# Gate and value of a SwiGLU block as 64-row products, one in each half of the PE array, issued in turn

## The chip, the cores and the metric

One Trainium2 chip, one of its cores. The metric is the time that the device takes for one execution of the program, in microseconds (us), the median of several runs.

## What is computed

The reference is an mLSTM cell over 4 batches, 8 heads, 768 tokens and 40 elements a head, and a SwiGLU block over the 3072 tokens of 320 elements that come out of it (8 heads x 40). All is fp32. Cut to what matters:

```python
for t in range(S):                                   # S = 768, in every batch and head
    m_new = np.maximum(f_gate[:, :, t] + m, i_gate[:, :, t])
    f_stab = np.exp(f_gate[:, :, t] + m - m_new)
    i_stab = np.exp(i_gate[:, :, t] - m_new)
    m = m_new
    C = f_stab * C + i_stab * outer(v[t], k[t])
    n = f_stab * n + i_stab * k[t]
    denom = np.maximum(np.abs(n @ q[t]), 1.0)
    y[:, :, t] = sigmoid(o_gate[:, :, t]) * (C @ q[t]) / denom

x = y.transpose(0, 2, 1, 3).reshape(3072, 320)
g = x @ w_gate                                       # 320 x 1536
out = (g * sigmoid(g) * (x @ w_val)) @ w_out         # 1536 x 320
```

The weights of the block come as fp64 and are rounded to fp32 on the chip.

## The kernel before

**The cell.** The 768 tokens of a batch are six chunks of 128. A chunk of a batch is a unit u, so there are 24, and a unit goes through five stages. `turn` (from L242) loads a later unit's k, q, v and o, and transposes k and q on TensorE (tp_kq, eight transposes, two tiles), which ACT copies to SBUF (kT, qT). Two heads lie in the two halves of the partitions, 64 rows each. `scores` (L256) multiplies kT and qT head by head: four matmuls with the lower 64 rows into one tile sp, then four with the upper 64 into another, each tile then weighted by DVE (s_sb). `attend` (L266) makes inter, add and intra and the state C. `rows` (L300) works out the denominators (den) on DVE and x_sb, the 128x320 output of the cell for the chunk: POOL multiplies (L310), DVE divides (L311). `seam` (L313) transposes x_sb on TensorE into tp_x, in three pieces of 128, 128 and 64 columns, and copies it into xT, whose partitions are then the 320 elements in chunks of 128, 128 and 64 (`kch`, L53): the first two pieces on ACT, the third on DVE (L324).

Before the first unit of a batch, `weigh` (L222) makes the weights between tokens: 48 matmuls of 32 rows (nm), DVE, a select on POOL, an exponential on ACT.

**The block.** A step `hidden(b, n, m)` (L334) makes 128 of the 1536 columns for half a batch (384 tokens): gate, three matmuls that add up in one PSUM tile gv_ps (128, 128 and 64 rows of the weights, 384 columns of xT), then value, three more in another gv_ps. ACT takes the sigmoid of the gate (L345), DVE multiplies twice (L346, L347) into h_sb. Twelve such steps make a half batch, then three steps `project` (L349), twelve matmuls each (o_ps), a copy on ACT and a store. So there are 96 hidden steps and 24 projections. A matmul of fp32 is recorded as two weight loads and two matmuls.

**The order.** The first batch's cell runs first, and between its stages the weights of the block come in (L212 to L217): 24 pieces, each a DMA and a chain of five DVE operations, one of ACT and an add on POOL (L209), which turns fp64 into fp32. Then each batch's 30 steps of the block run with the 30 stages of the next batch's cell among them, one after each step (L377 to L389); the last batch's steps run alone. A tile framework builds the program from this: it may move instructions on an engine, and sets the waits between engines.

**PSUM.** Eight banks, two for each of four tags: tr (tp_g, dec, tp_kq, tp_x), att (nm, sp), hp (inter, add, intra) and gen (gv_ps, o_ps).

Of the kernel before, what the change touches and what calls it, by code (L numbers as in the profile page):

```python
# [9 lines left out]
F32 = mybir.dt.float32  # L10
# [6 lines left out]
L = 128  # tokens of a chunk  # L17
# [4 lines left out]
def kernel(  # L22
# [24 lines left out]
    PR = H // 2  # pairs of heads, a head in each half of the partitions  # L47
# [5 lines left out]
    kch = [(d0, min(128, DM - d0)) for d0 in range(0, DM, 128)]  # L53
    NKC = len(kch)
    assert NB * L == S and NFC * 128 == DF and TW % 128 == 0 and TW <= 512 and D <= DP and BH <= 128
# [7 lines left out]
    psum = ctx.enter_context(tc.tile_pool(name="psum", bufs=2, space=PSUM))  # L63
# [47 lines left out]
    # which pair a row of the gates belongs to, and which half  # L111
# [6 lines left out]
    # a pair's state is kept whole; a head's own part of it is its half's columns  # L118
# [27 lines left out]
    # token on the partition: g_T[t, c, bh] and, for the chunks from the second, e_T  # L146
    g_T = const.tile([128, NB, BH], F32)
    e_T = const.tile([128, NB, BH], F32)
    for dst, src, c0 in ((g_T, g_sb, 0), (e_T, e_sb, 1)):
        tp = psum.tile([128, NB, BH], F32, name="tp_g", tag="tr")  # L150
# [4 lines left out]
    # the decay of a whole chunk, spread over the partitions of the state  # L155
# [3 lines left out]
    dec_ps = psum.tile([128, NB - 1, B * PR], F32, name="dec_ps", tag="tr")  # L159
# [8 lines left out]
    conv_scope = ExitStack()  # L168
    conv = conv_scope.enter_context(tc.tile_pool(name="conv", bufs=2))
    PW = 512  # L170
    NPW = max(PW, 2 * DM)

    def weight(dst, src):
        if src.dtype == F32:
            nc.scalar.dma_start(out=dst, in_=src)
            return
# [30 lines left out]
        if len(shape) == 3:  # L207
            sz, tf = (x.rearrange("p (a d) -> p a d", a=shape[1]) for x in (sz, tf))
# [211 lines left out]
```

## Time and profile before

| | us |
|---|---|
| median of 3 runs | 925.11 (924.93 to 929.82) |
| span of the profiled execution | 925.1 |
| PE busy | 875.6 |
| DVE busy | 337.9 |
| ACT busy | 156.1 |
| POOL busy | 120.8 |

The profile is that of one execution. PE is TensorE's matmuls, PEld its weight loads, which can lie under matmuls. A matmul's end is modelled, so that rows of neighbouring matmuls overlap by up to 0.2 us: durations in the timeline are best taken from start to start. The chain is followed back from the last instruction, each time to what released it. In rows of stages (windows) a pair such as 17.35 (x24) is busy time and records of PE, then of PEld where the row is of one source line, and the last three numbers are the granted share of TensorE's clock, the mean busy share of the DMA engines, and GB/s.

### The profile page before, as it was taken

To read this page: it belongs to the slowest core of one execution; us is meant where nothing else is said; L and a number is where in the kernel's file an instruction comes from. 1 tells how busy PE (TensorE), PEld (TensorE's weight loads), DVE (VectorE), ACT (ScalarE), POOL (GpSimd) and SP (SyncE) were. 2 spreads that over 40 slices of the span, in tenths; PEclk is the share of its full clock that TensorE was granted. 3 is DMA by queue.
4 is the path that set the end of the run, shared out by engine and by line. 5 is a ranking of instruction groups with operands and counts; after the bars stand their busy time and mean duration, and the time that the engine had idled before them with its cause. 6 is when DMAs were issued, how large, how long until landed. Compare 5 with 4: busy or idle time off the path is not lost.

```text
span 925.1 us, 8778 instructions
## 1 busy us (share of the span) xinstructions
PE 875.6 (95%) x3477; PEld 553.0 (60%) x3477; DVE 337.9 (37%) x625; ACT 156.1 (17%) x274; POOL 120.8 (13%) x127
## 2 busy tenths in 40 slices
PE   6856769999999999999999999999999999999998
PEld 5755557855665568755665568655755565445445
DVE  5588877433214322334213322234313321210220
ACT  2322122311111112311111112311111101100110
POOL 2344434400000001100000002100000000000000
PEclk9999855599999999799999998799999999999999
DMA  9244454011021111011111110011100000000000
GB/s 139 64 108 112 116 132 114 1 21 30 15 44 21 29 18 33 7 25 27 27 31 22 29 29 22 7 29 22 37 14 1 1 8 14 1 0 22 0 1 21
DMA packets 107273, 32.22 MB, mean 35 GB/s; under 512 B 100640, under 2 KB 103712, under 8 KB 107232
## 3 DMA queue, kind: packets, MB, share of 16 engines
q1 hardware_dynamic: 103392, 19.87, 12.0%
q10 hardware_dynamic: 3840, 11.80, 4.1%
q8 instruction: 27, 0.44, 0.2%
q14 instruction: 14, 0.11, 0.0%
HBM read 27.72 MB, written 3.93 MB: 34 GB/s over the span
## 4 chain that ended last, share of the span: by engine, by line
PE 92%; DVE 3%; issue 1%; DMA 1%; POOL 1%; ACT 0%; ACTq 0%; DVEq 0%; POOLq 0%
PE gv_ps L341 49%; PE o_ps L352 17%; PE nm L230 8%; PE intra L293 5%; PE sp L263 5%; PE inter L273 3%; PE tp_kq L252 3%; PE add L280 2%; PE tp_x L319 1%; DVE top L196 1%; POOL wv_sb L209 0%; DVE size L204 0%; DMA raw<-in_moe_w_gate_dram 0%; DVE top L195 0%; DVE power L203 0%
## 5 line engine op out<-in xcount | busy, mean ns | idle before, releaser
L341 PE MATMUL gv_ps<-xT,wg_sb 128*128 128x384 f32 (+1 forms) x576 | 237.4, 531 | 0.0
L341 PE MATMUL gv_ps<-xT,wv_sb 128*128 128x384 f32 (+1 forms) x576 | 233.5, 526 | 0.0
L341 PEld LDWEIGHTS gv_ps<-xT,wv_sb 128*128 128x128 f32 (+1 forms) x576 | 94.4, 190 | 130.2 <-issue 103.6
L352 PE MATMUL o_ps<-wo_sb,h_sb 128*128 128x320 f32 x576 | 159.3, 435 | 0.0
L341 PEld LDWEIGHTS gv_ps<-xT,wg_sb 128*128 128x128 f32 (+1 forms) x576 | 96.1, 194 | 99.8 <-issue 76.5
L352 PEld LDWEIGHTS o_ps<-wo_sb,h_sb 128*128 128x128 f32 x576 | 108.1, 190 | 44.7 <-issue 1.1
L346 DVE TENSOR_TENSOR sg<-sg,gv_ps 128x384 f32<-128x384 f32 x96 | 53.1, 553 | 221.7 <-ACT sg L345 221.7
L345 ACT ACTIVATE sg<-gv_ps 128x384 f32<-128x384 f32 x96 | 47.1, 490 | 335.7 <-PE gv_ps L341 335.6
L347 DVE TENSOR_TENSOR h_sb<-sg,gv_ps 128x384 f32<-128x384 f32 x96 | 53.2, 554 | 118.8 <-PE gv_ps L341 118.8
L230 PE MATMUL nm<-M_sb,nid 32*128 32x128 f32 x384 | 79.9, 395 | 2.1 <-DVE w_sb L232 1.1
L230 PEld LDWEIGHTS nm<-M_sb,nid 32*128 32x128 f32 x384 | 76.0, 300 | 5.8 <-DVE w_sb L232 3.6
L247 POOL TENSOR_TENSOR v_w<-va,w_sb 128x328 f32<-128x328 f32 x24 | 18.1, 752 | 315.0 <-PE add L280 254.3
L293 PEld LDWEIGHTS intra<-va,s_sb 128*128 128x128 f32 x384 | 54.2, 221 | 3.5 <-issue 0.3
L293 PE MATMUL intra<-va,s_sb 128*128 128x41 f32 x384 | 53.8, 306 | 0.0
L263 PEld LDWEIGHTS sp<-qT,kT 64*128 64x128 f32 x384 | 47.1, 228 | 10.8 <-ACT qT L254 4.8
L263 PE MATMUL sp<-qT,kT 64*128 64x128 f32 x384 | 48.6, 324 | 3.2 <-ACT qT L254 3.2
L232 DVE TENSOR_TENSOR w_sb<-nm,g_T 128x512 f32<-128x512 f32 x48 | 33.2, 691 | 39.6 <-PE nm L230 39.4
L310 POOL TENSOR_TENSOR x_sb<-o_sb,y_sb 128x320 f32<-128x320 f32 x24 | 20.8, 869 | 190.3 <-DVE y_sb L296 187.2
L252 PE MATMUL tp_kq<-ident,kq 128*128 128x128 f32 x192 | 34.1, 323 | 7.3 <-DVE xT L324 5.2
L319 PE MATMUL tp_x<-ident,x_sb 128*128 128x128 f32 (+1 forms) x72 | 14.9, 323 | 25.5 <-DVE x_sb L311 25.5
L252 PEld LDWEIGHTS tp_kq<-ident,kq 128*128 128x128 f32 x192 | 25.5, 164 | 20.6 <-issue 9.9
L234 POOL TENSOR_SCALAR_AFFINE_SELECT w_sb<-w_sb 128x1024 f32<-128x1024 f32 x24 | 26.6, 1108 | 82.5 <-DVE w_sb L232 82.5
(70 smaller groups left out, 494.3 us busy)
## 6 DMA issues: line engine op xcount, KB each, us to landing
kq<-in_k_dram SPq DMA_DIRECT2D x24, 160.0 KB, 3.0
kq<-in_q_dram SPq DMA_DIRECT2D x24, 160.0 KB, 2.8
va<-in_v_dram SPq DMA_DIRECT2D x24, 160.0 KB, 2.6
o_sb<-in_o_gate_dram SPq DMA_DIRECT2D x24, 160.0 KB, 2.6
raw<-in_moe_w_out_dram ACTq DMA_DIRECT2D x6, 640.0 KB, 4.0
out_dram<-z_sb SPq DMA_DIRECT2D x24, 160.0 KB, 1.8
raw<-in_moe_w_gate_dram ACTq DMA_DIRECT2D x6, 512.0 KB, 3.7
raw<-in_moe_w_val_dram ACTq DMA_DIRECT2D x6, 512.0 KB, 3.6
```

The lines of the kernel that those rows point to most:

```text
L230: nc.tensor.matmul(nm[:, j, :], lhsT=nid[:, row:row + 1].to_broadcast([BH, 128]), rhs=M_sb[:, c, :], start=True, stop=True)
L232: nc.vector.tensor_tensor(w[:, two], nm, g2[:, two].unsqueeze(2).to_broadcast([128, PR, L]), op=ALU.add)
L234: nc.gpsimd.affine_select(wf, wf, compare_op=ALU.is_ge, fill=NEG, base=0, pattern=[[0, H], [1, L]], channel_multiplier=-1)
L252: nc.tensor.transpose(tp[:, j, :], un["kq"][:, n, 2 * j:2 * j + 2, :].rearrange("p h d -> p (h d)"), ident)
L263: nc.tensor.matmul(sp[:, j, :], lhsT=un["kT"][r, j, :], rhs=un["qT"][r, j, :], start=True, stop=True)
L273: nc.tensor.matmul(inter[:, 2 * j:2 * j + 2, :].rearrange("p h d -> p (h d)"), lhsT=un["qT"][:, j, :], rhs=state["C"][:, j, :], start=True ...
L293: nc.tensor.matmul(intra[:, h, :], lhsT=un["s"][:, h % 2, h // 2, :], rhs=un["v"][:, h, :], start=True, stop=True)
L341: nc.tensor.matmul(p, lhsT=w_sb[0:dn, kc, ts(m, 128)], rhs=xts[b][0:dn, kc, ts(n, TW)], start=(kc == 0), stop=(kc == NKC - 1))
L345: nc.scalar.activation(sg, ps[0], AF.Sigmoid)
L346: nc.vector.tensor_tensor(sg, sg, ps[0], op=ALU.mult)
L347: nc.vector.tensor_tensor(hs[b, n][:, m, :], sg, ps[1], op=ALU.mult)
L352: nc.tensor.matmul(p, lhsT=hs[b, n][:, m, ts(i, 128)], rhs=wo_sb[:, m, :], start=(m == 0), stop=(m == NFC - 1))
```

## The change

Gate and value are no longer cut in pieces of 128, 128 and 64 rows but in five of 64. The gate's weights lie in partitions 0 to 63 of one tile wgv_sb, the value's in 64 to 127, so that a gate product uses the lower 64 rows of the array and a value product the upper 64. `hidden` takes both PSUM tiles at once and issues the two in turn, five pieces each. For that the tokens must lie in both halves of the partitions: `rows` copies x_sb on POOL into xx_sb, each group of 64 columns twice, and `seam` makes five transposes of 128 columns, in two PSUM tiles of four and one, both copied by ACT. The weights come in 12 pieces for gate and value together (128 partitions x 5 x 128, by two DMAs of 64 partitions each) and six for the third matrix, 18 for 24. PSUM has two tags of four banks: gen as before for gv_ps and o_ps, and cell for all else.

```diff
-    kch = [(d0, min(128, DM - d0)) for d0 in range(0, DM, 128)]
-    NKC = len(kch)
+    HP = 64
+    NKC = DM // HP
...
-    psum = ctx.enter_context(tc.tile_pool(name="psum", bufs=2, space=PSUM))
+    psum = ctx.enter_context(tc.tile_pool(name="psum", bufs=4, space=PSUM))
...
-    wg_sb = wpool.tile([128, NKC, DF], F32)
-    wv_sb = wpool.tile([128, NKC, DF], F32)
+    wgv_sb = wpool.tile([128, NKC, DF], F32)
...
-    PW = 512
-    NPW = max(PW, 2 * DM)
+    PW = 128
+    NPW = max(NKC * PW, 2 * DM)
...
-        for kc, (d0, dn) in enumerate(kch):
-            for sb, dram in ((wg_sb, moe_w_gate), (wv_sb, moe_w_val)):
-                pieces.append((sb[0:dn, kc, f0:f0 + PW], dram[d0:d0 + dn, f0:f0 + PW]))
+        src = [(slice(i * HP, (i + 1) * HP), w[:, f0:f0 + PW].rearrange("(c p) f -> p c f", p=HP))
+               for i, w in enumerate((moe_w_gate, moe_w_val))]
+        pieces.append((wgv_sb[:, :, f0:f0 + PW], src))
...
-            sp = psum.tile([128, PR, L], F32, name="sp", tag="att")
+            sp = psum.tile([128, PR, L], F32, name="sp", tag="cell")
...
+        xx = un["x"] = work.tile([128, NKC, 2, HP], F32, name="xx_sb")
+        nc.gpsimd.tensor_copy(xx, x.rearrange("p (c d) -> p c d", d=HP).unsqueeze(2).to_broadcast([128, NKC, 2, HP]))
...
-        tp = psum.tile([128, NKC, L], F32, name="tp_x", tag="tr")
-        for kc, (d0, dn) in enumerate(kch):
-            nc.tensor.transpose(tp[0:dn, kc, :], units[u]["x"][:, d0:d0 + dn], ident)
-        full = DM // 128
-        nc.scalar.copy(xts[b][:, 0:full, ts(c, L)], tp[:, 0:full, :])
-        if full < NKC:
-            dn = kch[-1][1]
-            nc.vector.tensor_copy(xts[b][0:dn, full, ts(c, L)], tp[0:dn, full, :])
+        for k0, k1 in ((0, 4), (4, NKC)):
+            tp = psum.tile([128, PR, L], F32, name="tp_x", tag="cell")
+            for kc in range(k0, k1):
+                nc.tensor.transpose(tp[:, kc - k0, :], units[u]["x"][:, kc, :, :].rearrange("p a d -> p (a d)"), ident)
+            nc.scalar.copy(xts[b][:, k0:k1, ts(c, L)], tp[:, 0:k1 - k0, :])
...
-        ps = []
-        for w_sb in (wg_sb, wv_sb):
-            p = psum.tile([128, TW], F32, name="gv_ps", tag="gen")
-            for kc, (_, dn) in enumerate(kch):
-                nc.tensor.matmul(p, lhsT=w_sb[0:dn, kc, ts(m, 128)], rhs=xts[b][0:dn, kc, ts(n, TW)],
+        ps = [psum.tile([128, TW], F32, name="gv_ps", tag="gen") for _ in range(2)]
+        for kc in range(NKC):
+            for i in range(2):
+                r = slice(i * HP, (i + 1) * HP)
+                nc.tensor.matmul(ps[i], lhsT=wgv_sb[r, kc, ts(m, 128)], rhs=xts[b][r, kc, ts(n, TW)],
                                  start=(kc == 0), stop=(kc == NKC - 1))
-            ps.append(p)
```

How the built program changes, at three places. First TensorE, from the scores of one unit of the second batch on (x3 means three matmuls; gv_ps is gate and value, of which the first row is the end of the step before). Before:

```order
L341 MATMUL gv_ps<-xT,wv_sb 128x384 x3
L263 MATMUL sp<-qT,kT 128x128 x8
L341 MATMUL gv_ps<-xT,wg_sb 128x384 x3
L341 MATMUL gv_ps<-xT,wv_sb 128x384 x3
L273 MATMUL inter<-C_sb,qT 128x82 x4
L280 MATMUL add<-v_w,kq_84 128x82 x4
L341 MATMUL gv_ps<-xT,wg_sb 128x384
L293 MATMUL intra<-va_87,s_sb 128x41 x8
```

The same stretch and what follows it, up to the next transposes of k and q, after:

```order
L261 MATMUL sp<-qT,kT 128x128 x8
L339 MATMUL gv_ps<-xT,wgv_sb 128x384 x10
L271 MATMUL inter<-C_sb,qT 128x82 x4
L278 MATMUL add<-v_w,kq_84 128x82 x4
L291 MATMUL intra<-va_87,s_sb 128x41 x8
L339 MATMUL gv_ps<-xT,wgv_sb 128x384 x20
L321 MATMUL tp_x<-ident,xx_sb 128x128 x5
L339 MATMUL gv_ps<-xT,wgv_sb 128x384 x10
L250 MATMUL tp_kq<-ident,kq_85 128x128 x8
```

A step is ten matmuls where it was six, no single gate product stands between add and intra any more, and two whole steps lie between intra and the transposes tp_x. With tile numbers, the ten of one step read so (a number is a PSUM tile, so the first is the gate's, the second the value's):

```order
L339 MATMUL gv_ps_1167<-xT_358,wgv_sb_105 128x384
L339 MATMUL gv_ps_1168<-xT_358,wgv_sb_105 128x384
L339 MATMUL gv_ps_1167<-xT_358,wgv_sb_105 128x384
L339 MATMUL gv_ps_1168<-xT_358,wgv_sb_105 128x384
L339 MATMUL gv_ps_1167<-xT_358,wgv_sb_105 128x384
```

Gate and value alternate product by product. In the third step, among the first batch's last stages, the order has five of the gate and then five of the value.

Second TensorE at the start of the program, where the gates are transposed (tp_g) and the first batch is weighed (nm). Before:

```order
L152 MATMUL tp_g<-ident,g_sb 128x32 x6
L230 MATMUL nm<-M_sb,nid 128x128 x11
L152 MATMUL tp_g<-ident,e_sb 128x32 x5
L230 MATMUL nm<-M_sb,nid 128x128
L160 MATMUL dec_ps<-dec_r,halves 128x80
L230 MATMUL nm<-M_sb,nid 128x128 x20
```

After:

```order
L152 MATMUL tp_g<-ident,g_sb 128x32 x6
L152 MATMUL tp_g<-ident,e_sb 128x32 x5
L160 MATMUL dec_ps<-dec_r,halves 128x80
L228 MATMUL nm<-M_sb,nid 128x128 x48
L250 MATMUL tp_kq<-ident,kq_83 128x128 x8
L261 MATMUL sp<-qT,kT 128x128 x8
```

All 48 products of the first weighing now stand behind the transposes of e_sb, and the first transposes of k and q behind all 48; before, they were mixed.

Third POOL, in the first batch's cell, where the adds of the weight pieces (L206, once L209) stand among the cell's operations. Before:

```order
L247 TENSOR_TENSOR v_w<-va_86,w_sb 128x328
L209 TENSOR_TENSOR wg_sb<-top,size 64x512
L288 TENSOR_TENSOR C_old<-C_sb,dec 128x328
L310 TENSOR_TENSOR x_sb<-o_sb,y_sb 128x320
L209 TENSOR_TENSOR wv_sb<-top,size 64x512
```

After:

```order
L245 TENSOR_TENSOR v_w<-va_86,w_sb 128x328
L286 TENSOR_TENSOR C_old<-C_sb,dec 128x328
L308 TENSOR_TENSOR x_sb<-o_sb,y_sb 128x320
L206 TENSOR_TENSOR wgv_sb<-top,size 128x5x128
L311 COPY xx_sb<-x_sb 128x640
```

The copy of x_sb is new, and in this stage an add of a weight piece stands before it on POOL.

More of the change, by code (lines that the diff above doesn't have):

```diff
@@ L249, in turn @@
         for n, name in enumerate(("kT", "qT")):
-            tp = psum.tile([128, PR, L], F32, name="tp_kq", tag="tr")
+            tp = psum.tile([128, PR, L], F32, name="tp_kq", tag="cell")
             for j in range(PR):
@@ L270, in attend @@
         if c > 0:
-            inter = psum.tile([128, H, D1], F32, name="inter", tag="hp")
+            inter = psum.tile([128, H, D1], F32, name="inter", tag="cell")
             for j in range(PR):
@@ L277, in attend @@
         if c + 1 < NB:
-            add = psum.tile([128, PR, 2 * D1], F32, name="add", tag="hp")
+            add = psum.tile([128, PR, 2 * D1], F32, name="add", tag="cell")
             for j in range(PR):
@@ L290, in attend @@
             state["C"] = new
-        intra = psum.tile([128, H, D1], F32, name="intra", tag="hp")
+        intra = psum.tile([128, H, D1], F32, name="intra", tag="cell")
         for h in range(H):
@@ L307, in rows @@
         nc.vector.reciprocal(den, den)
-        x = un["x"] = work.tile([128, DM], F32, name="x_sb")
+        x = work.tile([128, DM], F32, name="x_sb")
         x3 = x.rearrange("p (h d) -> p h d", d=D)
```

26 lines of the change are left out of this document (12 added, 14 removed).

## The prediction

> **What bounds the kernel now.** I read the page first (busy time, the chain that ended last), then the stages in windows, then the timeline of single stages.
>
> ```profile
> span 925.1 us, 8778 instructions
> PE 875.6 (95%) x3477; PEld 553.0 (60%) x3477; DVE 337.9 (37%) x625; ACT 156.1 (17%) x274; POOL 120.8 (13%) x127
> PEclk9999855599999999799999998799999999999999
> PE 92%; DVE 3%; issue 1%; DMA 1%; POOL 1%; ACT 0%; ACTq 0%; DVEq 0%; POOLq 0%
> PE gv_ps L341 49%; PE o_ps L352 17%; PE nm L230 8%; PE intra L293 5%; PE sp L263 5%; PE inter L273 3%; PE tp_kq L252 3%; PE add L280 2%; PE tp_x L319 1%; DVE top L196 1%; POOL wv_sb L209 0%; DVE size L204 0%; DMA raw<-in_moe_w_gate_dram 0%; DVE top L195 0%; DVE power L203 0%
> ```
>
> TensorE is 92% of the chain, and the gate and value products alone (gv_ps) are 49%. The median of the runs is 925.11 us and the profiled span 925.1, so the sum below is made on the span and needs no correction.
>
> The products by stage (PE busy, records, granted clock):
>
> ```profile
> 0.00:186.00 186.00, 17.35 (x24) 6.24 (x24) 0.79 0.44 98
> 771.18:925.10 153.92, 111.61 (x288) 46.62 (x288) 1.00 0.02 8
> ```
>
> A hidden step (one m: gate and value) leaves 12 records, since each fp32 product is recorded as two loads and two matmuls: 2 products x 3 pieces x 2. So 2 of the 96 steps run before 186.00, 24 after 771.18 with no cell among them (288/12), and 70 between, among the cell's stages. Steps between other stages:
>
> ```profile
> 204.06 2.29 PE L341 MATMUL gv_ps<-xT,wg_sb 128*128 128x384 f32 x6
> 208.61 1.10 PE L252 MATMUL tp_kq<-ident,kq 128*128 128x128 f32 x8
> 209.54 2.29 PE L341 MATMUL gv_ps<-xT,wg_sb 128*128 128x384 f32 x6
> 214.00 1.60 PE L263 MATMUL sp<-qT,kT 64*128 64x128 f32 x16
> 215.54 2.40 PE L341 MATMUL gv_ps<-xT,wg_sb 128*128 128x384 f32 x6
> 220.19 1.12 PE L273 MATMUL inter<-C_sb,qT 128*128 128x82 f32 x8
> 771.18 2.29 PE L341 MATMUL gv_ps<-xT,wg_sb 128*128 128x384 f32 x6
> 826.91 19.65 PE L352 MATMUL o_ps<-wo_sb,h_sb 128*128 128x320 f32 x72
> ```
>
> From start to start a step takes 4.55, 4.46 or 4.65 us (204.06 to 208.61, 209.54 to 214.00, 215.54 to 220.19), and the twelve from 771.18 to 826.91 take 55.73, 4.64 each. I use 4.60 for the 70.
>
> **What a record costs.** Two neighbouring looks at the timeline without a change of row count, then three groups of weight loads:
>
> ```profile
> 508.25 0.81 PE L341 MATMUL gv_ps<-xT,wg_sb 128*128 128x384 f32 x2
> 508.57 0.81 PE L341 MATMUL gv_ps<-xT,wg_sb 128*128 128x384 f32 x2
> 240.32 0.29 PEld L341 LDWEIGHTS gv_ps<-xT,wg_sb 64*128 64x128 f32 x2 [0.55 <-issue]
> 241.16 0.94 PEld L341 LDWEIGHTS gv_ps<-xT,wv_sb 128*128 128x128 f32 x4 [0.55 <-issue]
> 242.65 0.29 PEld L341 LDWEIGHTS gv_ps<-xT,wv_sb 64*128 64x128 f32 x2 [0.55 <-issue]
> ```
>
> Undisturbed records start 0.32 us apart; I take 0.322. Where the row count changes, more passes: the two 64-row records take 0.84 (240.32 to 241.16) and the four 128-row records 1.49 (241.16 to 242.65). Together that is 2.33 where six records would be 1.93: a pair of changes, 64 rows in and out, costs 0.40. The idle 0.55 of the weight loader ends at each such change: the load is no longer hidden there. Each step has two such pairs, 0.80 of its 4.64.
>
> **Do two halves run side by side?** The change lives on this. The old trace shows it in the scores, eight matmuls (16 records) of 64 rows, first four in the lower half, then four in the upper. Two short looks:
>
> ```profile
> 512.71 1.60 PE L263 MATMUL sp<-qT,kT 64*128 64x128 f32 x16
> 512.82 0.38 PE L263 MATMUL sp<-qT,kT 64*128 64x128 f32 x2
> 513.37 0.39 PE L263 MATMUL sp<-qT,kT 64*128 64x128 f32 x4
> 514.24 2.40 PE L341 MATMUL gv_ps<-xT,wg_sb 128*128 128x384 f32 x6
> ```
>
> At 513.00 two records are in flight, at 513.55 four, with the same spread of starts (0.38 and 0.39 us with the tail): for a while the halves work at once at full pace, weight loads included. Issued in blocks of eight, they overlap only where the blocks meet; issued in turn, they can overlap all along.
>
> **The change, part by part.**
>
> 1. A step now has 10 products of 64 rows, 20 records, 10 in each half: 10 x 0.322 = 3.22 us if the halves overlap. Row changes are paid only where a run of 64-row work starts and ends. In the new order the 70 steps stand in 47 runs (eight in each twelve steps, one less at the start; scores join the run beside them), the last 24 in 2.
> Among the cells: 70 x 4.60 = 322.0 before; 70 x 3.22 + 47 x 0.40 = 244.2 after: **-77.8**. The last 24: 2 x 55.73 = 111.5 before; 24 x 3.22 + 0.8 = 78.1 after: **-33.4**.
> Bounds: 0.320 to 0.325 a record gives -2 to +3 (96 x 10); a run at 0.20 (only one side is paid) to 0.50 (the second half pays its first load after the first) gives -10 to +5.
>
> 2. Five transposes instead of three. The next eight of 128 columns go from 208.61 to 209.54, 0.116 each: 18 units after 186 us x 2 x 0.116 = +4.2. The scores' 1.54 (214.00 to 215.54) held their change of rows, 0.20, now counted with the runs: 18 x 0.20 = -3.6. Together **+0.6**.
>
> 3. A POOL copy of 128x640 between x_sb and the transposes, its length not in this trace. The nearest by size:
>
> ```profile
> L288 POOL TENSOR_TENSOR C_old<-C_sb,dec 128x328 f32<-128x328 f32 x16 | 12.1, 759 | 4.8 <-DVE C_sb L289 4.8
> L234 POOL TENSOR_SCALAR_AFFINE_SELECT w_sb<-w_sb 128x1024 f32<-128x1024 f32 x24 | 26.6, 1108 | 82.5 <-DVE w_sb L232 82.5
> L209 POOL TENSOR_TENSOR wo_sb<-top,size 128x640 f32<-128x640 f32 x6 | 11.2, 1861 | 14.6 <-DVE size L204 14.6
> 525.15 0.49 DVE L311 TENSOR_TENSOR x_sb<-x_sb,den 128x320 f32<-128x320 f32 x1
> 531.78 0.55 PE L319 MATMUL tp_x<-ident,x_sb 128*128 128x128 f32 x3
> ```
>
> So 0.75 to 1.86, and I take 1.1, as of the one-input 128x1024. Among the cells it is covered: x_sb is ready at 525.64 and needed at 531.78, after two steps. With two steps of 3.22 for 4.65 some 3.3 us are left, more than any bound. Were the cover gone, 18 x 1.1 = 20 us would return.
>
> 4. DVE and ACT per step:
>
> ```profile
> L345 ACT ACTIVATE sg<-gv_ps 128x384 f32<-128x384 f32 x96 | 47.1, 490 | 335.7 <-PE gv_ps L341 335.6
> L346 DVE TENSOR_TENSOR sg<-sg,gv_ps 128x384 f32<-128x384 f32 x96 | 53.1, 553 | 221.7 <-ACT sg L345 221.7
> L347 DVE TENSOR_TENSOR h_sb<-sg,gv_ps 128x384 f32<-128x384 f32 x96 | 53.2, 554 | 118.8 <-PE gv_ps L341 118.8
> ```
>
> 0.49 + 0.55 + 0.55 = 1.6 us, under the 3.22 of the next step. With four gen banks a pair is written again only two steps later: cost nothing. The four cell banks turn over nine tiles a unit, and a bank comes back only after three others; nothing there waits long.
>
> 5. The first stage, up to 186 us, which TensorE does not fill:
>
> ```profile
> 7.48 5.06 PE L230 MATMUL nm<-M_sb,nid 32*128 32x128 f32 x22 [0.96 <-DVE M_sb L139]
> 16.34 8.82 PE L230 MATMUL nm<-M_sb,nid 32*128 32x128 f32 x40
> 25.09 0.47 PE L252 MATMUL tp_kq<-ident,kq 128*128 128x128 f32 x1
> 35.73 3.10 PE L263 MATMUL sp<-qT,kT 64*128 64x128 f32 x16
> PE tp_x L319 <- DVE x_sb L311: 25.5, 5, 5.3
> PE tp_kq L252 <- DVE xT L324: 5.2, 4, 2.2
> ```
>
> The nm products now all stand behind the transposes of e_sb: 96 x 0.219 (8.75 for 40, from 16.34 to 25.09) = 21.0, to 37.4. The clock is half of the later one here (the scores' 16 take 3.10, later 1.60), so a transpose takes twice 0.116, 0.23. With 8 of these, 1.9, and an ACT copy of 512 columns behind them (0.6, an estimate from the 0.49 of 384 above) the first scores start near 39.9, not 35.73: +4.2. The wait for DVE's xT copy goes with the copy: -5.2. The POOL copy has no cover here (TensorE waits 25.5 us for x_sb already): 6 x 1.1 = +6.6. Twelve more transposes of 0.23: +2.8. Two steps at half clock, twice 4.6 before and twice 3.22 + 0.40 now: -2 each, -4. Sum **+4.4**, from -6 (fewer conversion pieces, 18 for 24, shorten the waits on DVE) to +12 (the copy at 1.86 and behind a weight piece).
>
> Sum: 925.1 - 77.8 - 33.4 + 0.6 + 4.4 = 818.9, **819 us**.
>
> **A rule against it.** The rows above have a record of the second half in flight before the first half's last one has started: in strict order its first could start only with the eighth, 7 x 0.11 after 512.71, and its own eighth at about 514.37, yet the next product stands at 514.24. The Trainium skill, TensorE: Matmul & The Clock Gate (Part 3: Packing small matmuls, The mechanism), says that matmuls start and end in program order; by these rows they don't. By that rule the sum would be 16 us higher, as in rival A.
>
> **The rivals.**
>
> A. The halves overlap but start in order. Each product is two records, so a half could start only beside the other's second: the pace stays, and each run ends one record later, 49 x 0.32 = +16: 835 us. Against it speak the scores' rows. Chance 0.08.
>
> B. The next weights are not loaded behind the running matmul when halves alternate. Then each record costs what the two behind a row change cost, 0.84/2 = 0.42: 4.2 a step. 70 x 4.2 + 18.8 = 312.8 (-9.2), 24 x 4.2 + 0.8 = 101.6 (-9.9), +5.0: 911 us. For it speaks that every first 64-row record in the trace shows its load; against it, four scores in flight at full pace. Chance 0.06. The same page (Measured speedup vs the span model) gives 3.07 for four row tiles, 77% of ideal; an estimate by it would be 20 x 0.322/1.54 = 4.2 a step, the same end. No row here shows such a loss.
>
> C. Slower: the halves take turns in the long accumulating products, because something that the short scores don't load (384 columns streaming for both, two banks accumulated at once) serves one half. The place is the gv step: 20 x 0.322 = 6.44. 70 x 6.44 + 18.8 = 469.6 (+147.6), 24 x 6.44 + 0.8 = 155.4 (+43.9), +5.0: 1122 us. It decides from 0.43 us a record and half on (a step of 4.3 with its share of runs). Chance 0.06.
>
> D. The change doesn't do what it says, because the program issues the halves in blocks. In the new order they stand in turn, except in the third step, among the first cells. Chance 0.01, with the time of C or a little less.
>
> **How the numbers follow.** Forecast 0.79, A 0.08, B 0.06, C 0.06, D 0.01. Predicted: 819. Low end: 819 less 11 (first stage), 10 (runs) and 2 (pace), not all at once: 800. High end: A's 835 with 7 (first stage), 5 (runs) and 3 (pace) is 850. That holds the forecast and A, 0.87 less some tail. Under 0.5%, about 4.6 us, a measurement of this kernel can't tell a change: faster is forecast, A and B, 0.93; slower C and D, 0.07 less 0.01 for what lies between.
>
> **What would show it.** A step in the last stretch starts 3.2 us after the one before (A: the same; B: 4.2; C: 6.4), with twice as many gv_ps records in flight as before. The stretch before the last projections is about 39 us, not 55.73. PE still 90% or more of the chain, no wait of tp_x for POOL after the first stage, the wait of tp_kq for DVE gone, first scores near 40 us. I am wrong if the step is over 4 us, or if TensorE shows idle time before gv_ps.

## The result and the profile after

| | before | after |
|---|---|---|
| median, us | 927.47 (924.93 to 933.5, 4 runs) | 804.53 (801.92 to 810.48, 4 runs) |
| ratio, 95% interval | | 0.866 [0.861, 0.871] |
| span of the profiled execution, us | 925.1 | 802.8 |

The kernel is 13% faster; 819 us were forecast, 800 to 850 as the range. The page of the changed kernel, the lines that answer to the first ones quoted of the kernel before:

```profile
span 802.8 us, 10446 instructions
PE 750.8 (94%) x4293; PEld 549.6 (68%) x4293; DVE 329.1 (41%) x571; ACT 161.8 (20%) x292; POOL 132.4 (16%) x145
PEclk9999997559999999789999999689999999999999
PE 91%; DVE 4%; issue 1%; POOL 1%; ACT 0%; ACTq 0%; DVEq 0%; POOLq 0%
PE gv_ps L339 40%; PE o_ps L349 20%; PE nm L228 9%; PE intra L291 6%; PE sp L261 5%; PE tp_kq L250 3%; PE inter L271 3%; PE add L278 3%; PE tp_x L321 2%; DVE top L195 1%; POOL xx_sb L311 1%; DVE top L194 1%; DVE top L198 0%; DVE size L203 0%; POOL wgv_sb L206 0%
```

TensorE still sets the end. It has more matmul records than before (4293 for 3477) and less busy time, and gv_ps has fallen from 49% of the chain to 40% of a shorter one.

To see where the 122.3 us of span went, cut both executions at the same two points: at the first `add` of the second batch's first unit, when three of the 96 hidden steps are done in both kernels, and at the start of the last 24 steps. Windows of the kernel before, then of the changed one:

```profile
0.00:191.68 191.68, 145.51 (x603) 122.07 (x603) 131.14 (x230) 51.10 (x74) 72.86 (x69) 0.80 0.42 95
191.68:771.18 579.50, 579.50 (x2444) 357.10 (x2444) 179.88 (x346) 90.14 (x169) 47.97 (x58) 0.97 0.11 22
771.18:925.10 153.92, 150.60 (x434) 73.81 (x432) 26.88 (x49) 14.90 (x32) 0.00 (x0) 1.00 0.02 8
```

```profile
0.00:181.13 181.13, 132.31 (x640) 117.59 (x640) 128.48 (x194) 49.01 (x73) 70.48 (x69) 0.86 0.53 100
181.13:682.62 501.49, 501.49 (x3032) 358.53 (x3031) 173.96 (x329) 97.69 (x188) 61.97 (x76) 0.97 0.13 26
682.62:802.80 120.18, 117.02 (x625) 73.46 (x624) 26.62 (x48) 15.10 (x32) 0.00 (x0) 1.00 0.03 10
```

The last stage gives 33.7 us (153.92 to 120.18), the stage with cell and block mixed 78.0 (579.50 to 501.49), the first stage 10.6 (191.68 to 181.13). In the middle stage TensorE is busy without a gap in both kernels, so its 78 us are TensorE time saved and nothing else.

The timeline of the changed kernel, some steps among the cell's stages and the first twelve of the last 24:

```profile
207.71 6.72 PE L339 MATMUL gv_ps<-xT,wgv_sb 64*128 64x384 f32 x40
214.36 0.77 PE L321 MATMUL tp_x<-ident,xx_sb 128*128 128x128 f32 x5
215.05 3.50 PE L339 MATMUL gv_ps<-xT,wgv_sb 64*128 64x384 f32 x20
218.48 1.09 PE L250 MATMUL tp_kq<-ident,kq 128*128 128x128 f32 x8
219.50 3.50 PE L339 MATMUL gv_ps<-xT,wgv_sb 64*128 64x384 f32 x20
222.83 1.60 PE L261 MATMUL sp<-qT,kT 64*128 64x128 f32 x16
224.37 5.92 PE L349 MATMUL o_ps<-wo_sb,h_sb 128*128 128x320 f32 x21
...
682.62 38.97 PE L339 MATMUL gv_ps<-xT,wgv_sb 64*128 64x384 f32 x240
721.52 2.69 PE L349 MATMUL o_ps<-wo_sb,h_sb 128*128 128x320 f32 x9
```

A lone step takes 3.43 us (215.05 to 218.48), two in a row 6.65 (207.71 to 214.36), and the first twelve of the last 24 take 38.90 (682.62 to 721.52), 3.24 each, where they took 55.73. In 38.90 us stand 240 records of 64 rows: 0.162 us each, half of the 0.322 at which one half of the array runs. In the trace's records the two products of a pair start 7 ns apart, from the first pair on.

TensorE's waits that the change was to move:

```profile
PE tp_x L321 <- POOL xx_sb L311: 30.5, 6, 6.9
```

All six waits of the token transposes lie in the first stage, one in each of its six units. Among the later cells the copy is covered. The wait of tp_kq for DVE's copy into xT is gone.

### The profile page after: what moved, and what is told of

Same layout as the page of the kernel before. It is cut to its first block, busy times and chain, and to the rows that moved or that the text cites. A ratio compares the mean times of both kernels' runs of the same rounds, so it can differ in the third digit from the quotient of the medians.

```text
span 802.8 us, 10446 instructions
## 1 busy us (share of the span) xinstructions
PE 750.8 (94%) x4293; PEld 549.6 (68%) x4293; DVE 329.1 (41%) x571; ACT 161.8 (20%) x292; POOL 132.4 (16%) x145
## 4 chain that ended last, share of the span: by engine, by line
PE 91%; DVE 4%; issue 1%; POOL 1%; ACT 0%; ACTq 0%; DVEq 0%; POOLq 0%
PE gv_ps L339 40%; PE o_ps L349 20%; PE nm L228 9%; PE intra L291 6%; PE sp L261 5%; PE tp_kq L250 3%; PE inter L271 3%; PE add L278 3%; PE tp_x L321 2%; DVE top L195 1%; POOL xx_sb L311 1%; DVE top L194 1%; DVE top L198 0%; DVE size L203 0%; POOL wgv_sb L206 0%
## 5 line engine op out<-in xcount | busy, mean ns | idle before, releaser
L339 PE MATMUL gv_ps<-xT,wgv_sb 64*128 64x384 f32 x1920 | 344.4, 497 | 0.0
L339 PEld LDWEIGHTS gv_ps<-xT,wgv_sb 64*128 64x128 f32 x1920 | 191.3, 190 | 117.5 <-issue 12.3
L228 PE MATMUL nm<-M_sb,nid 32*128 32x128 f32 x384 | 76.0, 390 | 0.0
L291 PEld LDWEIGHTS intra<-va,s_sb 128*128 128x128 f32 x384 | 51.5, 215 | 1.1 <-DVE top L198 1.1
L261 PE MATMUL sp<-qT,kT 64*128 64x128 f32 x384 | 46.0, 309 | 4.3 <-ACT qT L252 4.3
L321 PE MATMUL tp_x<-ident,xx_sb 128*128 128x128 f32 x120 | 21.4, 318 | 30.5 <-POOL xx_sb L311 30.5
L321 PEld LDWEIGHTS tp_x<-ident,xx_sb 128*128 128x128 f32 x120 | 15.6, 160 | 41.1 <-POOL xx_sb L311 33.3
L352 ACT COPY z_sb<-o_ps 128x320 f32<-128x320 f32 x24 | 10.2, 426 | 137.2 <-PE o_ps L349 137.2
L234 ACT ACTIVATE w_sb<-w_sb 128x1024 f32<-128x1024 f32 x24 | 25.4, 1057 | 54.7 <-POOL w_sb L232 54.7
L301 ACT ACTIVATE o_sb<-o_sb 128x320 f32<-128x320 f32 x24 | 11.2, 468 | 114.0 <-DMA o_sb<-in_o_gate_dram 114.0
```

Of the source, the lines that this page charges most:

```text
L228: nc.tensor.matmul(nm[:, j, :], lhsT=nid[:, row:row + 1].to_broadcast([BH, 128]), rhs=M_sb[:, c, :], start=True, stop=True)
L234: nc.scalar.activation(wf, wf, AF.Exp)
L261: nc.tensor.matmul(sp[:, j, :], lhsT=un["kT"][r, j, :], rhs=un["qT"][r, j, :], start=True, stop=True)
L291: nc.tensor.matmul(intra[:, h, :], lhsT=un["s"][:, h % 2, h // 2, :], rhs=un["v"][:, h, :], start=True, stop=True)
L321: nc.tensor.transpose(tp[:, kc - k0, :], units[u]["x"][:, kc, :, :].rearrange("p a d -> p (a d)"), ident)
L339: nc.tensor.matmul(ps[i], lhsT=wgv_sb[r, kc, ts(m, 128)], rhs=xts[b][r, kc, ts(n, TW)], start=(kc == 0), stop=(kc == NKC - 1))
```

## The experiments

The theory is that two products in different halves of the array run at the same time for their whole length, and that the rest of the gain of a step is saved changes between 128-row and 64-row work. The rivals are that the gain comes from the order of the products alone, from the PSUM banks, or from fewer changes of row count. All times by step are from start to start over the first twelve of the last 24 steps, where nothing else runs on TensorE; "the twelve" below are these. Experiments 1, 2, 3 and 5 have one run each.

**1. Both in one half.** The value products read the gate's weights and the lower copy of the tokens, so the value is not the reference's; counts, shapes, order and banks stay.

```diff
-                r = slice(i * HP, (i + 1) * HP)
+                r = slice(0, HP)
```

> Value's products use the lower half too (they read the gate's weights and the tokens' lower copy, so value is not the reference's); 64 rows, number and order of products unchanged. Theory (the gain is the two halves at once): 20 records one after another, 6.45 us a step, 805 + 96 x 3.2 = 1112. In the first stage the scores of the fourth and fifth unit take 3.1 us again, if it is both halves at work that brings the full clock there. Rival 1 (the gain is the row changes that went): 3.3 us a step. Rival 2 for the first stage (denser issue brings the clock): scores of 1.6 to 2.1 there as in the changed kernel.

Measured: 1363.25 us. The page's clock strip, then the timeline:

```profile
PEclk9999555555999955555599995555559999999999
```

```profile
227.58 13.17 PE L339 MATMUL gv_ps<-xT,wgv_sb 64*128 64x384 f32 x20
240.67 1.97 PE L250 MATMUL tp_kq<-ident,kq 128*128 128x128 f32 x8
...
335.45 8.31 PE L349 MATMUL o_ps<-wo_sb,h_sb 128*128 128x320 f32 x24
...
360.73 6.71 PE L339 MATMUL gv_ps<-xT,wgv_sb 64*128 64x384 f32 x20
367.38 1.09 PE L250 MATMUL tp_kq<-ident,kq 128*128 128x128 f32 x8
...
1163.91 77.66 PE L339 MATMUL gv_ps<-xT,wgv_sb 64*128 64x384 f32 x240
1241.51 3.77 PE L349 MATMUL o_ps<-wo_sb,h_sb 128*128 128x320 f32 x13
```

The twelve take 77.60 us, 6.47 a step, against 3.24: twice, with the same instructions. So the second half of the array, and nothing else, takes 3.2 us off a step. With 96 steps longer by 3.23 the span of 802.8 would have become 1113; it is some 250 us longer still, because the clock stands at half for three long stretches (the 5s of the strip), in which a step takes 13.09 us (227.58 to 240.67) where it takes 6.65 at the full clock (360.73 to 367.38). What that says is taken up at the end. The expectation also had an idea for the first stage, that both halves at work bring the full clock there; it does not hold for the fifth unit, whose scores take 1.54 us here too (130.07 to 131.60), as at full clock.

**2. Gate first, then value.** The loops change places, so five products of one half are followed by five of the other.

```diff
-        for kc in range(NKC):
-            for i in range(2):
+        for i in range(2):
+            for kc in range(NKC):
```

> Gate's five products first, then value's five; all else as in the changed kernel. Theory (the halves work at once, and a half starts only when about three records of the other half that stand before it are still waiting, as in the scores): value's first record starts with gate's seventh of ten, so a step in the last stretch takes 12 records, 3.9 us, and a step that stands alone 16, 5.2 us; in all about 120 us more than the changed kernel, 925. Rival 1 (halves overlap in whatever order they are issued): 3.24 us a step, 805. Rival 2 (without turns nothing overlaps): 6.4 us a step, about 1110.

Measured: 960.84 us (one run, against 925.28 for the kernel before on the same chip). The timeline:

```profile
203.98 5.53 PE L339 MATMUL gv_ps<-xT,wgv_sb 64*128 64x384 f32 x20
209.44 1.09 PE L250 MATMUL tp_kq<-ident,kq 128*128 128x128 f32 x8
...
815.77 50.52 PE L339 MATMUL gv_ps<-xT,wgv_sb 64*128 64x384 f32 x240
866.23 2.15 PE L349 MATMUL o_ps<-wo_sb,h_sb 128*128 128x320 f32 x7
```

A step of the twelve takes 4.21 us (50.46/12), far from the 6.47 of one half: the halves overlap where the blocks meet. A lone step among the cells takes 5.46 (203.98 to 209.44), more than the 4.60 of the kernel before, since its first block begins and its second ends without a partner; so the whole is slower than before the change, with all of the change in it but the order of two loops. Two short looks at that stretch, at 821.58 to 821.90 and at 822.70:

```profile
821.25 0.81 PE L339 MATMUL gv_ps<-xT,wgv_sb 64*128 64x384 f32 x2
822.22 0.91 PE L339 MATMUL gv_ps<-xT,wgv_sb 64*128 64x384 f32 x4
```

Two records are in flight while one half works, four where two blocks meet. In the single records, ten of a half start 0.322 us apart, and the next half's first one starts beside the seventh of the half before it (821.906 beside 821.900, with the last of that half at 822.868); its second follows after 0.427 instead of 0.322. So half a step repeats every 2.045 us, and 24 halves with 1.2 for the last four records make 50.3. The expectation had the start beside the seventh right, but not the 0.427 behind it, nor the price of a lone step (5.2), and so was 36 us low. The order thus decides how much overlaps, and the forecast's use of the scores as a sign of it was sound in kind; how far the array reached ahead had to be measured.

**3. Turns of two products.** Two of the gate, two of the value, and so on.

```diff
-        for kc in range(NKC):
-            for i in range(2):
+        for kc, i in [(k, i) for k0 in range(0, NKC, 2) for i in range(2) for k in range(k0, min(k0 + 2, NKC))]:
+            if True:
```

> Turns of two products, two of gate, two of value, two, two, one, one. Theory (about three records of look-ahead): with the first of gate's four records started three are waiting, so value starts beside it; 3.24 us a step, 805 +- 4. Rival (the turn must be product by product): the second half starts two records late in each run, +0.65 us a run, 835, or does so at every turn, 3.9 us a step.

Measured: 806.68 us, and in the timeline:

```profile
684.51 39.07 PE L339 MATMUL gv_ps<-xT,wgv_sb 64*128 64x384 f32 x240
723.52 2.69 PE L349 MATMUL o_ps<-wo_sb,h_sb 128*128 128x320 f32 x9
```

39.01 us, 3.25 a step, nothing lost against single turns. That fits the reach seen in experiment 2: two products are four records.

**4. The new banks alone.** The kernel before, with four banks each for the tags cell and gen.

```diff
-    psum = ctx.enter_context(tc.tile_pool(name="psum", bufs=2, space=PSUM))
+    psum = ctx.enter_context(tc.tile_pool(name="psum", bufs=4, space=PSUM))
...
-        tp = psum.tile([128, NB, BH], F32, name="tp_g", tag="tr")
+        tp = psum.tile([128, NB, BH], F32, name="tp_g", tag="cell")
```

> The kernel before with the new PSUM tags alone (four banks for gv_ps and o_ps, four for the cell). Theory (banks are only what lets the halves take turns; in the first stage they remove the 5.2 us wait of the transposes for DVE's copy): 915 to 922, ratio 0.99 to 1.0; a step stays at 4.64 us. Rival (the banks are what made the first stage 10 us shorter): first products of the second batch's first add at 181 instead of 192 us, 910 to 914.

Measured: 912.36 us, ratio 0.9821 [0.977, 0.9871], against 0.866 for the whole change. The twelve take 55.74 us, as before. So the banks do nothing for a step of the old kind. They give some 10 us early: at its first `add` of the second batch, 190.34, 58 records of 12, 4.8 steps, are done where the kernel before has 3.0 at 191.68; 1.3 us and 1.8 steps of 4.6 are 9.8 us. That is more than the expectation allowed (915 to 922); its rival had the time, 910 to 914, but not the place, an `add` at 181.

**5. The old banks under the new products.** The changed kernel with two banks for each of the four old tags.

```diff
-    psum = ctx.enter_context(tc.tile_pool(name="psum", bufs=4, space=PSUM))
+    psum = ctx.enter_context(tc.tile_pool(name="psum", bufs=2, space=PSUM))
...
-            tp = psum.tile([128, PR, L], F32, name="tp_x", tag="cell")
+            tp = psum.tile([128, PR, L], F32, name="tp_x", tag="tr")
```

> The changed kernel with the old PSUM tags, two banks each, so that one pair of gate and value is all there is. Theory: the next pair waits for ACT and DVE, 0.49 + 0.55 + 0.55 and some 0.3 between them, so a step in the last stretch takes 3.24 + 1.3 to 1.9 = 4.6 to 5.1 us; among the cells stages cover a part. In all 880 to 930. Rival (the banks only matter to the cell's tiles): 805 to 812, with the wait of the transposes for the copy of xT back in the first stage.

Measured: 913.25 us (a single time). Timeline of the first three of the twelve steps, then a row of the waits:

```profile
756.30 3.53 PE L339 MATMUL gv_ps<-xT,wgv_sb 64*128 64x384 f32 x20
760.96 4.15 PE L339 MATMUL gv_ps<-xT,wgv_sb 64*128 64x384 f32 x20 [1.13 <-DVE sg L343]
765.64 4.15 PE L339 MATMUL gv_ps<-xT,wgv_sb 64*128 64x384 f32 x20 [0.54 <-DVE sg L343]
```

```profile
PE gv_ps L339 <- DVE sg L343: 24.8, 30, 2.4
```

A step takes 4.68 us (760.96 to 765.64): the 3.24 of the products and most of the 1.6 that ACT and DVE need to empty the pair, one after the other. With the gate and the value started together both banks are occupied until the products end, and the next pair has nowhere to go. The row of waits shows a part of it: the gate's first product goes on as soon as its own bank is free and the value's must wait longer (760.96 and 761.62), so that the ten take 4.15 us where the first ten took 3.53. The new products without the four gen banks would thus have gained nothing in a step (4.64 before). The banks alone give 2%, the products alone about 1% (913.25 for some 925), both together 13%.

**6. One run of 64-row work a step.** The kernel before with the new banks; the four 128-row products come first, then both 64-row products, in the same half.

```diff
-        ps = []
-        for w_sb in (wg_sb, wv_sb):
...
+        order = [(i, kc) for i in range(2) for kc in range(NKC - 1)] + [(i, NKC - 1) for i in range(2)]
+        for i, kc in order:
```

> The old pieces of 128, 128 and 64 rows and the new PSUM tags; gate's and value's 128-row products first, then both 64-row ones (both in the lower half), so that a step has one pair of row changes instead of two and nothing overlaps. Theory: 12 x 0.322 + 0.2 to 0.4 = 4.1 to 4.3 us a step, 0.35 to 0.55 less than before; with the banks 875 to 890, ratio 0.945 to 0.96: of the 1.40 us that a step gained about a third is row changes, two thirds the overlap. Rival (the row changes are the gain): 3.4 us a step, 810.

Measured: 883.46 us, ratio 0.9495 [0.944, 0.955]. The timeline of one step:

```profile
740.34 1.46 PE L341 MATMUL gv_ps<-xT,wg_sb 128*128 128x384 f32 x4
741.63 1.45 PE L341 MATMUL gv_ps<-xT,wv_sb 128*128 128x384 f32 x4
743.01 0.91 PE L341 MATMUL gv_ps<-xT,wg_sb 64*128 64x384 f32 x2
743.76 0.81 PE L341 MATMUL gv_ps<-xT,wv_sb 64*128 64x384 f32 x2
744.50 1.56 PE L341 MATMUL gv_ps<-xT,wg_sb 128*128 128x384 f32 x4
```

The twelve steps take 51.03 us, 4.25 each: 12 records at 0.322, 3.86, and 0.39 for one pair of changes. Against 4.64 with two pairs, a pair costs 0.39, as the forecast had read it. This splits the 1.40 that a step gains: 0.78 are two pairs of row changes, and 0.64 are two record times (12 to 10, since ten records in each half at once do the work of 12 in a row).

**7. The copy on ACT.** The changed kernel, with the doubled copy of the tokens on ACT instead of POOL.

```diff
-        nc.gpsimd.tensor_copy(xx, x.rearrange("p (c d) -> p c d", d=HP).unsqueeze(2).to_broadcast([128, NKC, 2, HP]))
+        nc.scalar.copy(xx, x.rearrange("p (c d) -> p c d", d=HP).unsqueeze(2).to_broadcast([128, NKC, 2, HP]))
```

> The changed kernel with the copy of x_sb on ACT instead of POOL. Theory (the copy is covered among the cells and bare in the first stage, where it stands behind an add of a weight piece on POOL in some units): the six waits of tp_x, 30.5 us, shrink by 0.3 us each and 1.7 us in two or three of them, 3 to 7 us in all; 798 to 802. Rival (it isn't on the path): 804 +- 2.

Measured: 805.22 us, ratio 0.8655 [0.8608, 0.8701]: no difference from the change itself (0.866 [0.861, 0.871]) that the runs can tell; 798 to 802 were expected, and the rival's 804 came. The copy costs nothing among the cells, wherever it runs. In its profiled execution the waits of tp_x in the first stage are 18.6 us for 30.5, and the first stage is 8.8 us shorter; of that 3.7 are left at the end of the span. The cut between the stages hides some of the rest: the clock comes back at 184.2 here, 12 us behind the cut at 172.30, where in the changed kernel it is back at 177.9, before the cut at 181.13.

**8. The scores in turn.** The changed kernel, with the scores' eight products issued one in the lower, one in the upper half.

```diff
+        sps = [psum.tile([128, PR, L], F32, name="sp", tag="cell") for _ in range(2)]
+        for j in range(PR):
+            for two in range(2):
+                r = slice(two * DP, two * DP + DP)
+                nc.tensor.matmul(sps[two][:, j, :], lhsT=un["kT"][r, j, :], rhs=un["qT"][r, j, :], start=True, stop=True)
```

> The changed kernel with the scores' eight products issued in turn, lower and upper half. Theory (same mechanism in short products): the 16 records take 8 x 0.111 = 0.89 us instead of 1.33 at full clock, 0.44 x 19 units, and 1.0 us less at half clock in five units: 13 us less, 790 to 793. Rival (scores are covered elsewhere or short products don't gain): 804 +- 2.

Measured: 792.24 us, ratio 0.8538 [0.8485, 0.8592], 12 us less than the change. In the timeline the scores of a unit at full clock:

```profile
79.30 1.16 PE L261 MATMUL sp<-qT,kT 64*128 64x128 f32 x16 [0.68 <-ACT qT L252]
80.39 1.12 PE L272 MATMUL inter<-C_sb,qT 128*128 128x82 f32 x8
```

They take 1.09 us (79.30 to 80.39), where they took 1.54 (222.83 to 224.37). The order of issue alone, with not one product more or fewer, gives that: what experiment 2 took away, this adds at the other place with 64-row work. In the profiled executions 9.9 of 17.0 us lie in the middle stage and 7.1 in the first, where the clock differs as well.

**9. Four row groups.** The changed kernel, with the 32-row products nm issued in turn for four tiles, each in other rows; the small gate tensors are held four times over.

```diff
-                    nc.tensor.matmul(nm[:, j, :], lhsT=nid[:, row:row + 1].to_broadcast([BH, 128]), rhs=M_sb[:, c, :],
-                                     start=True, stop=True)
+                    for n in range(4):
+                        r = slice(n * BH, (n + 1) * BH)
+                        row = b * H + 2 * j + n % 2
+                        nc.tensor.matmul(nms[n][:, j, :], lhsT=nid[r, row:row + 1].to_broadcast([BH, 128]),
+                                         rhs=M_sb[r, c + n // 2, :], start=True, stop=True,
+                                         tile_position=(n * BH, 0))
```

> The changed kernel with one more use of the same idea: the products nm (32 rows deep) are issued in turn for four PSUM tiles, each tile from another 32 rows of the array, where all of them lay in rows 0 to 31; the small gate tensors are held four times over for that. The theory (what ends in the gain is that row groups without a row in common take their records at once, whatever the depth of the product) says: the block of 12 nm tiles, 17.1 to 20.8 us a batch in the changed kernel, falls to what VectorE needs to empty twelve tiles, 12 x 0.69 = 8.3 us, and at best 8.5 to 11; three blocks stand between the feed-forward steps with nothing beside them on TensorE, so 25 to 36 us go, and a few more in the first stage: 765 to 780 us. The rival (the halves overlap only as two halves, or short records are held by their weight loads): the block keeps 17 us and more, 800 to 806 us.

Measured: 765.64 us, ratio 0.827 [0.8225, 0.8316]. The block of the third batch in the changed kernel, then in this one:

```profile
327.34 17.12 PE L228 MATMUL nm<-M_sb,nid 32*128 32x128 f32 x96
```

```profile
302.68 1.96 PE L233 MATMUL nm<-M_sb,nid 32*128 32x128 f32 x32
304.56 0.91 PE L347 MATMUL gv_ps<-xT,wgv_sb 64*128 64x384 f32 x2
...
312.53 5.09 PE L347 MATMUL gv_ps<-xT,wgv_sb 64*128 64x384 f32 x16
```

The block takes 9.85 us (302.68 to 312.53) with four records of a step among it, for 17.05 (327.34 to 344.39), and its first 32 records, four tiles, take 1.88 (302.68 to 304.56), 0.059 each. VectorE empties a tile in 0.68, twelve in 8.2, so VectorE now sets much of the pace: the four banks come free at that rate, and the second 32 records follow the first only at 305.40. In the profiled executions the nm records take 40 us less in all, counted from start to start, of the 41 by which the span is shorter.

**10. All together.** Experiments 7, 8 and 9, and the transposes of a unit's end and of the next unit's start in one stage, so that fewer runs of 64-row work are cut.

```diff
+        for u in us:
+            groups += [[(f, u)] for f in (scores, attend, rows)] + [[(seam, u)]]
+            if u + 1 in us:
+                groups[-1].append((turn, u + 1))
```

> The products nm in four row groups, the scores issued in turn in both halves, the token copy on ScalarE, and the cell steps grouped so that a unit's seam and the next unit's turn come in one step (fewer changes between 128-row and 64-row work). If the parts add up: about 12 us less than with the nm products alone for the scores (24 pairs, some 0.6 us of TensorE saved each, and the first stage), nothing for the copy, and some 15 changes of row group at about 0.2 us, 3 us, for the grouping: 750 to 766 us. If VectorE and the banks become the limit inside the steps instead, within 5 us of the run with the nm products alone.

Measured: 749.09 us (748.61 to 753.71), ratio 0.8095 [0.8054, 0.8136]: 19% below the kernel before, and 55 us below the change. The parts add up: 38.9 for nm, and 16.5 where 15 were expected for the rest.

## Why the forecast came out as it did

**The hidden step (part 1): right.** 3.22 a step was forecast for the overlapped halves and 3.24 measured, run changes included; the last 24 steps gave 33.7 us for 33.4. Same-half (6.47) shows that the overlap is the cause, and the step of 4.25 with one run that a pair of row changes costs 0.39.

**The price of a run: somewhat too high.** The forecast took 0.40 for each of 47 runs, bounds 0.20 to 0.50. In the timeline above a lone step takes 3.43 and a pair 6.65, so 0.21 stand in the run itself (over 3.22 and 6.44); with scores joined (219.50 to 224.37 is 4.87, of which 3.22 and 1.34) it is 0.31. The way in is paid before the run: the 128-row record in front of it, the last of the five tp_x or of the eight tp_kq, takes 0.20 until the run starts, where the others of its kind take 0.11. So a run costs 0.30, and 0.40 with scores. The 0.40 for all is right where 64-row work of one half lies between 128-row work, as in experiment 6; where both halves start together, a quarter of it is gone.

**The transposes (part 2): right but for the way into a run.** Five tp_x take 0.69 (214.36 to 215.05), where three took 0.39 before: 0.30 for the forecast 0.23. The eight tp_kq take 1.02 (218.48 to 219.50) where they took 0.93. The 0.09 of the way in is most of both differences.

**The middle stage as a whole: near, partly by luck.** It came out 2 us below its forecast (78.0 for some 76, which is 69 of the 70 steps and the +0.6 of part 2). Counted from the start of one record to the start of the next, gate and value take 83.7 us less, where the forecast has 76.7 for 69 steps and their runs. Against these 7 us stand 5.8 that the forecast had too little elsewhere: the transposes take 7.0 more for 4.2, intra, now in front of runs, 1.7 more for nothing, and the scores 2.3 less for 3.6. The nm products take 0.7 less.

**The copy (part 3) and the engines behind a step (part 4): right.** The copies of the first stage take 0.85 to 1.25 us, within the bounds of 0.75 and 1.86; the covered ones take 0.72, under them. No wait for it stands among the later cells, and moving it changes nothing. "With four gen banks a pair is written again only two steps later: cost nothing" holds, and experiment 5 shows what it would cost with two: 1.4 us of every step. That the change needs its banks was said in one sentence; it deserved a price.

**The first stage (part 5): the term that was mis-sized.** To the first `add` of the second batch the forecast's terms make +3.3 (the sum -106.2, less -76.1 and -33.4); measured were -10.6. This is 14 us, more than its own bound of -6 allowed, and it is nearly the whole distance from 819 to 804.5. Step by step it began as forecast: the first scores stand at 40.83 (39.9 forecast), and the wait for the copy is there, 30.5 us where DVE's x_sb had 25.5. What failed is the sentence "the clock is half of the later one here": it was taken for the whole stage in both kernels. The scores of the fourth and the fifth unit and the fifth's intra, in the kernel before and in the changed one:

```profile
97.85 2.93 PE L263 MATMUL sp<-qT,kT 64*128 64x128 f32 x16
...
118.26 3.10 PE L263 MATMUL sp<-qT,kT 64*128 64x128 f32 x16 [0.67 <-ACT qT L254]
...
124.79 3.55 PE L293 MATMUL intra<-va,s_sb 128*128 128x41 f32 x16
```

```profile
101.75 2.08 PE L261 MATMUL sp<-qT,kT 64*128 64x128 f32 x16
...
118.40 1.61 PE L261 MATMUL sp<-qT,kT 64*128 64x128 f32 x16
...
121.79 1.92 PE L291 MATMUL intra<-va,s_sb 128*128 128x41 f32 x16
```

The trace tells the granted clock from its first change on; before that the strip and the rows show full clock, though the scores take the 3.1 us of half clock there. In the changed kernel the clock is full from 102.8 to 113.0, during the fourth unit, at half for the 3.4 us around the next transposes, and full again from 116.4 to 130.1, for the fifth; in the kernel before it is full for 3.4 us only (106.2 to 109.6) until 188.1. The two units take 33.6 us from transpose to transpose (97.35 to 130.99), for 43.2 before (90.32 to 133.49). In the fifth, scores, inter and add take 3.4 us (118.40 to 121.79) for 6.5 (118.26 to 124.79), and intra 1.9 for 3.6: 4.8 us. In the fourth the scores take 0.9 less, inter and add 0.8 each: 2.5 us.

Over the whole stage the windows above say where the 10.6 us are: TensorE is busy for 13.2 us less (145.51 to 132.31) and waits for 2.7 us more. Counted from start to start:

| TensorE in the first stage, change in us | forecast | measured |
|---|---|---|
| scores, inter, add, intra, tp_kq, as many records as before | 0 | -10.0 |
| three steps of gate and value | -5.1 | -3.5 |
| twelve more transposes tp_x | +2.8 | +2.7 |
| waits, nm and a little else | +5.6 | +0.2 |

The forecast's -5.1 are its -4 for two steps and the 1.1 that one of the 70 gains; its 5.6 are +4.2, -5.2 and +6.6. Measured are 2.7 more of waits and 2.6 less of nm, whose 192 records now stand in two blocks. So some 10 of the 14 us are the clock, and most of the rest is in the forecast's waits and the place of nm. No run changes the clock alone: this share is read from the traces and was not tried. That the total still lies in the range is owed to the low end's 12 us for runs and pace, which were not needed there. Which units run at full clock differs from kernel to kernel:

| kernel | of the six units, at full clock from the scores on | first `add` of the second batch | steps done by then |
|---|---|---|---|
| before | none | 191.68 | 3.0 |
| same-half | one | 195.15 | 3.0 |
| new banks alone | two | 190.34 | 4.8 |
| the change | two | 181.13 | 3.0 |
| gate first, then value | two | 184.77 | 3.0 |
| old banks under the new products | three | 181.36 | 3.0 |
| the change, two in turn | three | 178.54 | 3.0 |
| the change, copy on ACT | four | 172.30 | 3.3 |

More units at full clock go with a shorter first stage (a step of same-half is twice as long, a lone one of gate first 2 us longer, and the row of the new banks alone has 1.8 steps more in it), but not in every row: the old banks under the new products have three units and no shorter stage than the change has with two. The new banks alone bring it about, and so do the new products with the old banks, so it belongs to neither part of the change by itself. Why the clock comes up in one unit and not in the next was not settled.

**The rivals.** A, starts in strict order, is refuted twice: the products stand 7 ns apart, and in experiment 2 a half starts beside the seventh of ten records that stand before it in the program, three of which begin later. In strict order half a step would repeat every 2.9 us (nine records), not every 2.045. The Trainium skill, TensorE: Matmul & The Clock Gate (Part 3: Packing small matmuls, The mechanism), says that matmuls keep program order in start and end; across halves of the array this trace does not agree, with that 2.045. B, weight loads that are not hidden, would have shown 4.2 a step, C, halves in turns, 6.4; 3.24 was measured. D is out with them.

## What to carry over

Products that use 64 rows or fewer cost as much as those that use 128 (0.32 us a record of 384 columns in both), but two in different halves run at once if they are issued in turn, and four in different quarters overlap too: order them so before cutting anything else, since reordering existing products alone gave 12 us here and four row groups 39. Started together they also end together, so they need PSUM banks for two rounds; with banks for one the whole gain went into waiting for ACT and DVE. Where TensorE has gaps, don't forecast a stage at one clock: price the stage at both, and let the range hold the difference.

## What the runs showed of the hardware

- Different row groups run out of program order by a few records: four records of the one half, two fp32 products, stand beside the first four of the other (experiments 2 and 3).
- A stream of 64-row work in one half didn't bring the clock back. In same-half the strip falls to 5 around each block of the 32-row nm, and steps of 13.09 us follow for some 150 us, with short 128-row work of the cell between them and TensorE busy all the while; the full clock is back during the 24 records of 128-row projections at 335.45. In its first stage the clock came up once, at 127.1, behind 3.0 us of 128-row transposes (123.49 to 126.46). It didn't drop by itself either: the 77.60 us of the twelve steps run at full clock with one half in use. In the changed kernel, with both halves in use, the clock is back within a step: behind the block of nm that ends at 344.39 one step takes 5.46 us and the next lone one 3.33.
- 32-row records in four groups take 0.059 us each over the 32 of four tiles, at full clock. In one group they take 0.112 at full clock (the first 36 of the block at 327.34) and 0.213 at half clock (its last 59), 0.178 over the block. At the same clock four groups thus make 1.9 times the pace over such a short stretch, not four times; in its middle eight records start at four to 0.112 us. Most of the 7 us that the block gains is the clock: at 0.112 throughout, its 96 records in one group would take 10.8 us (an estimate from that row), and the 9.85 include four records of a step.
- The 128-row record in front of 64-row work takes 0.20 us where its like take 0.11, so a part of the price of a change of rows is recorded ahead of the change.
